# A new order of the opening work, later output projections, and one numerator moved out of the gate/up chunks

## The chip, the cores and the metric

The kernel runs on one core of a Trainium2 chip. The metric is the time of one execution on the device, in microseconds (us). The program is one instruction stream per engine: TensorE (PE) for matmuls, VectorE (DVE), ScalarE (ACT), GpSimd (POOL) and SyncE (SP), which issues most DMAs. Each engine takes its instructions in order, and the engines meet at semaphores.

## The reference

One token mixer and one feed-forward network read the same `x` (2048 tokens, 640 features), and a gate per token mixes them. Cut to what matters:

```
g = sigmoid((x * gate_w).sum(-1))
q, k, v = split(x @ wqkv)                    # 32 heads of 20
pq, pk = q @ w_phi[h], k @ w_phi[h]          # 20 x 20 for each head
phi = [softmax(p), softmax(-p)]              # for q and for k
kv, z = sum over tokens of phi_k * v, and of phi_k
o = (phi_q @ kv) / (phi_q @ z + 1e-6)
a = o @ wo
b = (gelu(x @ w_gate) * (x @ w_up)) @ w_down # 1728 hidden features
out = g * a + (1 - g) * b
```

The attention is linear: `kv` and `z` are sums over all tokens, so every key has to be done before the first output of attention.

## The kernel before, in words

Tokens are cut into 16 tiles of 128 and four slabs of 4 tiles. There are four stages, in an order written out by hand; a small helper (`_Sched`) adds to each instruction the semaphore waits that its buffers need. Everything below is issued from one Python loop, so the order of the calls is the order on each engine.

*Loads and start* (`loads`, then `attention_state` to its first `gram`). SyncE issues x for the first slab, the five row blocks of the v weights (L239), and then, one after the other, DMA transposes: x for tiles 4 and 5 (L224), the k weights `wkT` (L220), x for tiles 6 and 7, the q weights `wqT`, and x for the rest. ScalarE's queue loads `w_phi` (L235) and `gate_w` (L240). GpSimd makes the masks. VectorE multiplies `w_phi` with the masks into a block-diagonal `BD` (L307). TensorE does v of the first slab in steps by weight rows (L366), turns `gate_w` into a column (L316, copied by VectorE at L318), and does v of tiles 4 to 7 (`v_early`) and the keys of tiles 0 to 3 (`k_early`). `fold(kt, "k" or "q", banks, engine)` multiplies `w_phi` into the weights (L334): 6 matmuls into a pair of PSUM banks, then a copy by VectorE or ScalarE (L347, L349). A `k_early` needs all five k folds, a `pq` all five q folds. `proj` is the matmul loop behind them (its matmuls are recorded at L354).

*State* (the rest of `attention_state`). For each tile: keys and v, exponentials on ScalarE (L416), and on VectorE `k_norm`: sums over the 20 features of a head (L427), a reciprocal (L431), and two products (L436). `gram(t)` adds the tile to `kv` and `z` in PSUM banks 3 and 4 (L452), and `pq` makes the exponentials of the queries (`Eq`, L521). In this stage, once `columns` is set, a matmul is split into two halves of 64 columns.

*Gate/up* (`gateups`). For each slab 14 chunks of hidden features: 5 matmuls for gate and 5 for up (L354), gelu on ScalarE (L629), a product on VectorE (L631). During slab 0 the state is finished (`state`). During slab 1, after chunks 4 and 8, the *numerators* of tiles 0 and 1 are computed. A numerator `num(t)` is 20 matmuls into banks 2 to 5 (L657), a chain of eleven VectorE instructions (L673 to L686) that divides by the denominators and ends in `Og`, and a DMA transpose on SyncE's queue to `goT` (L689).

*Down* (`downs`). Tiles are done in pairs (`down_pair`). The contraction of 64 + 64 rows is split in two row halves that run side by side, one tile in each: a *step* is two matmuls (L713), one for each tile of the pair, in two different banks. The output columns are done in two parts of 320 (three parts of 256, 256 and 128 for the last pair), and each part has a first and a second half of the rows, so a pair has four *legs* (last pair: six). A leg is 14 steps (second half: 13) over `w_down`, followed by 5 steps over `wo`, which read `goT`. The second half's legs write the same banks as the first half's with rows exchanged, so they first wait for TensorE's own semaphore (`after=[("turn", bank)]`) of the first. Then the part is scaled by the gate and copied out (L726, L724), and the pair is stored (L737). A pair is 74 steps. `downs` counts the steps of a slab and places numerators after given ones: steps 1, 31, 61 and 91 of slab b carry tiles 4b+2 to 4b+5.

Of the kernel before, what the change touches and what calls it, by code (L numbers as in the profile page):

```python
# [3 lines left out]
P = 128  # L4
# [103 lines left out]
class _Kernel:  # L108
    S, D, H, DH, F = 2048, 640, 32, 20, 1728
# [98 lines left out]
    def loads(self):  # L208
# [13 lines left out]
        def xturn(t, n):  # L222
# [43 lines left out]
        for i in range(KD):  # L266
            n = self.HHI[i] - self.HLO[i] + 1
            base = P * i - DH * self.HLO[i]
            m = self.mask[:, i, 0:n]
            pool(lambda e, m=m: e.memset(m, 1.0), [("mask", i)])  # L270
            pool(lambda e, m=m, n=n, base=base: e.affine_select(
                m, m, pattern=[[-DH, n]], compare_op=ALU.is_ge, fill=0.0, base=base, channel_multiplier=1),
                [("mask", i)])
            pool(lambda e, m=m, n=n, base=base: e.affine_select(
                m, m, pattern=[[DH, n]], compare_op=ALU.is_ge, fill=0.0, base=DH - 1 - base, channel_multiplier=-1),
                [("mask", i)])
        for r in (0, 1):
# [143 lines left out]
            reads=[("ps", b0 + 1)], writes=[("gcol", t)])  # L421

    def k_norm(self, t):
        sc = self.sc
        se = t % self.NSE
        H, DH = self.H, self.DH
        sc.op("dve", lambda e: e.tensor_reduce(  # L427
            self.Dk[:, se, 0, :].rearrange("p (s h) -> p s h", h=H),
            self.Ek[:, se, :, :].rearrange("p s (h d) -> p s h d", d=DH), AX.X, ALU.add),
            reads=[("Ek", se, 0), ("Ek", se, 1)], writes=[("Dk", se)])  # L430
        sc.op("dve", lambda e: e.reciprocal(self.Dk[:, se, 1, :], self.Dk[:, se, 0, :]),  # L431
              reads=[("Dk", se)], writes=[("Rk", se)])
        for s in (0, 1):
            v = self.Ek[:, se, s, :].rearrange("p (h d) -> p h d", d=DH)
            r = self.Dk[:, se, 1, s * H:(s + 1) * H].unsqueeze(2).to_broadcast([P, H, DH])
            sc.op("dve", lambda e, v=v, r=r: e.tensor_tensor(v, v, r, ALU.mult),  # L436
                  reads=[("Rk", se)], writes=[("Ek", se, s)])
# [97 lines left out]
    def attention_state(self):  # L535
        NT = self.NT
        order = [(b, i) for b in range(self.NB) for i in range(self.KD)]
        sc = self.sc
        ones = self.nc.const_aps.tensor(1.0, [P, 512], BF16)
        for n in (512, 512, 512, 512, 512, 512, 128):  # L540
            sc.op("pe", lambda e: e.matmul(self.bank(0, n), ones[:, 0:P], ones[:, 0:n], start=True, stop=True),
                  writes=[("ps", 0)])
        vs, ve, xt = self.v_step, self.v_first_evac, self.x_transpose
        xt(0, 6, "d")
        xt(1, 7, "a")
        xt(2, 2, "d")
# [48 lines left out]
        for t in range(4, NT):  # L595
            if t < 8:
                self.k_early(t, 1)
            else:
                self.vk(t)
            self.k_norm(t)  # L600
            m = 2 * t - 2 if t < 8 else t + 5
            while n < m:
                if n == m - 1:
                    for g in range(g, t - 2):
                        self.gram(g)
                    g = t - 2
                self.pq(order[n][0], order[n][1], n)
                n += 1
# [80 lines left out]
        sc.dma("sp", lambda e: e.dma_start_transpose(self.goT[:, gs, :, :], self.Og[:, sl, :]),  # L689
               reads=[("Og", sl)], writes=[("goT", gs)], guard=old)  # L690

    def down_pair(self, t0, banks, widths):

        sc = self.sc
        ts = (t0, t0 + 1)
# [3 lines left out]
        last = t0 + 2 == self.NT  # L699
        os_ = t0 % 4  # L700

        def mm(r, j, h, c, opens, x, n):
            t = ts[j]
            tt, gs, bk, w0, a = t % 4, t % 8, banks[h][j], sum(widths[:h]), 64 * r
            w, end = widths[h], x == n - 1
# [7 lines left out]
            sc.op("pe", lambda e: e.matmul(self.bank(bk, w), lhs, rhs, start=opens and x == 0, stop=end and not opens,  # L713
                                           skip_group_check=True),
                  reads=rd, writes=[("ps", bk)] + ([("turn", bk)] if end else []), signal=end,
                  after=[("turn", bk)] if x == 0 and not opens else ())

        def evac(h):
            w0, w = sum(widths[:h]), widths[h]
# [17 lines left out]
            sc.dma("sp", lambda e: e.dma_start(rows[:, :, c0:c1], self.outsb[:, os_:os_ + 2, c0:c1]),  # L737
                   reads=[("outsb", os_ + j, k) for j in (0, 1) for k in hs], writes=[("out", t0, h)])

        for q in range(2 * nw):  # L740
            h, opens = q % nw, q < nw
            cs = list(range(NFC + 1 if opens else NFC)) + [NFC + 1 + k for k in range(KD)]
            for x, c in enumerate(cs):
                for r in (0, 1):
                    mm(r, r if opens else 1 - r, h, c, opens, x, len(cs))
                if x == len(cs) - 1 and not opens:
# [8 lines left out]
    def ffn(self):  # L755
# [10 lines left out]
        def downs(b, side):  # L766
            p = [pairs[(self.pn + k) % 2] for k in (0, 1)]
            n = 0
            for t in (4 * b, 4 * b + 2):
                final = t + 2 == self.NT  # L770
                for _ in self.down_pair(t, p + [(2, 3)] if final else p, (256, 256, 128) if final else (320, 320)):
                    n += 1
                    if n in side:
                        self.num(side[n])
# [69 lines left out]
```

The softmax here doesn't subtract the row's maximum and nothing guards it: scores larger than these inputs give would overflow.

## Time and profile before

| what | value |
|---|---|
| median of 8 runs | 287.98 us (287.43 to 288.28) |
| the profiled execution's own time | 288.28 us |
| its span, first to last instruction | 287.0 us |
| TensorE busy, loads and start, 0 to 29.60 us | 27.33 us of 29.60 |
| TensorE busy, state, 29.60 to 85.41 us | 55.81 us of 55.81 |
| TensorE busy, gate/up, 85.41 to 198.04 us | 111.73 us of 112.63 |
| TensorE busy, down, 198.04 to 284.20 us | 86.09 us of 86.16 |
| after the last matmul | 2.80 us |
| VectorE busy in the down stage | 55.73 us of 86.16 |
| granted TensorE clock | 1.00 throughout |

How to read it: all lines come from one profiled execution on the chip. A line of the timeline has the start, the busy time, engine, source line, operation, out<-in, and in brackets how long the engine was idle before and what ended that. The chain that ended last is the path from the last instruction back to whatever released it; "issue" in it is time in which the engine waited for nothing that the profile shows. SPq is SyncE's queue of DMA issues. A busy TensorE is not one at its peak, since matmuls overlap and their ends are modelled (a matmul of 512 columns is shown with 379 ns, but 50 of them take 10.74 us in the chain, 215 ns each); a few matmuls are missing from the records.

### The profile page before, as it was taken

The numbers are of one execution on the slowest core, as the hardware profiler recorded it, in microseconds if no ns is written. First come the engines' busy times: TensorE is split into PE (matmuls) and PEld (weight loads), VectorE is DVE, ScalarE is ACT, GpSimd is POOL, SyncE is SP. The second block draws the span as 40 slices with busy tenths as digits, with TensorE's granted clock in tenths as the row PEclk, the third lists the DMA queues.
The fourth block names the chain that finished last, engine by engine and source line by source line (L and its number), as shares of the span: only waits on it lengthen the run. The fifth ranks groups of instructions, "written<-read, shape, count | busy, mean of one in ns | idle before, by whom it ended". The sixth has DMA issues, their size and how long they took to land.

```text
span 287.0 us, 7005 instructions
## 1 busy us (share of the span) xinstructions
PE 281.0 (98%) x3017; PEld 185.8 (65%) x3032; DVE 174.8 (61%) x353; ACT 104.5 (36%) x199; POOL 5.3 (2%) x36
## 2 busy tenths in 40 slices
PE   8989999999999999999999999999999999999995
PEld 4666689999994444444444444445777777777785
DVE  1338999999977553567242334225883883883801
ACT  3357887677663322322323223321112112112111
POOL 7000000000000000000000000000000000000000
PEclk9999999999999999999999999999999999999999
DMA  8999994000002000011000000000232333332221
GB/s 220 211 199 273 362 365 143 0 2 2 2 0 48 0 0 0 3 24 23 2 0 0 0 2 0 0 2 0 26 93 62 34 48 94 48 55 83 53 72 48
DMA packets 36938, 18.67 MB, mean 65 GB/s; under 512 B 28971, under 2 KB 36395, under 8 KB 36907
## 3 DMA queue, kind: packets, MB, share of 16 engines
q1 hardware_dynamic: 36240, 18.19, 25.7%
q8 instruction: 24, 0.39, 0.6%
q10 hardware_dynamic: 666, 0.03, 0.2%
q14 instruction: 8, 0.06, 0.1%
HBM read 9.04 MB, written 2.62 MB: 41 GB/s over the span
## 4 chain that ended last, share of the span: by engine, by line
PE 93%; SPq 3%; DMA 2%; issue 1%; ACT 0%
PE ps L354 60%; PE ps L713 28%; PE ps L657 2%; DMA xT<-in_A_x_dram 2%; PE ps L452 2%; SPq L220 1%; PE ps L334 1%; SPq L239 1%; SPq L224 1%; SPq L216 0%; ACT outsb L726 0%
## 5 line engine op out<-in xcount | busy, mean ns | idle before, releaser
L354 PE MATMUL ps<-xT,wg_sb 128*128 128x512 bf16 (+1 forms) x265 | 63.8, 379 | 0.4 <-issue 0.2
L354 PE MATMUL ps<-xT,wu_sb 128*128 128x512 bf16 (+1 forms) x263 | 63.3, 379 | 0.5 <-DVE hT L631 0.2
L629 ACT ACTIVATE gl<-ps 128x512 bf16<-128x512 f32 x52 | 30.9, 596 | 73.1 <-PE ps L354 68.7
L631 DVE TENSOR_TENSOR hT<-ps,gl 128x512 bf16<-128x512 f32 x39 | 26.7, 690 | 38.3 <-PE ps L354 38.3
L713 PE MATMUL ps<-wd_sb,hT 64*128 64x320 bf16 x648 | 49.4, 296 | 0.0
L354 PEld LDWEIGHTS ps<-xT,wu_sb 128*128 128x128 bf16 (+1 forms) x270 | 26.5, 99 | 29.8 <-DVE hT L631 0.5
L354 PEld LDWEIGHTS ps<-xT,wg_sb 128*128 128x128 bf16 (+1 forms) x270 | 26.2, 99 | 29.0 <-ACT gl L629 0.2
L354 PE MATMUL ps<-w,xT 128*64 128x512 bf16 (+6 forms) x398 | 41.6, 325 | 1.1 <-DMA xT<-in_A_x_dram 0.9
L726 ACT ACTIVATE outsb<-ps,Gm 128x320 bf16<-128x320 f32 (+2 forms) x31 | 14.5, 515 | 72.4 <-PE ps L713 72.4
L354 PEld LDWEIGHTS ps<-w,xT 128*64 128x64 bf16 (+1 forms) x400 | 35.6, 107 | 6.0 <-DMA xT<-in_A_x_dram 1.1
L713 PEld LDWEIGHTS ps<-wd_sb,hT 64*128 64x128 bf16 x648 | 31.0, 94 | 12.2 <-issue 0.4
L713 PE MATMUL ps<-wo_sb,goT 64*128 64x320 bf16 (+2 forms) x340 | 27.8, 288 | 0.0
L354 PE MATMUL ps<-xT,wq 128*64 128x512 bf16 (+1 forms) x184 | 25.9, 380 | 0.1
L436 DVE TENSOR_TENSOR Ek<-Ek,Dk 128x640 bf16<-128x640 bf16 x32 | 25.0, 821 | 0.6
L684 DVE TENSOR_TENSOR O<-ps,RH 128x640 bf16<-128x640 f32 x32 | 24.8, 815 | 0.0
L427 DVE TENSOR_REDUCE Dk<-Ek 128x64 f32<-128x1280 bf16 x16 | 23.7, 1478 | 0.0
L416 ACT ACTIVATE Ek<-ps 128x640 bf16<-128x640 f32 x32 | 20.7, 703 | 3.5 <-PE ps L354 3.5
L521 ACT ACTIVATE Eq<-ps 128x512 bf16<-128x512 f32 x40 | 21.6, 607 | 0.7 <-PE ps L354 0.4
L631 DVE TENSOR_TENSOR xT<-ps,gl 128x512 bf16<-128x512 f32 x13 | 9.0, 691 | 18.2 <-PE ps L354 18.2
L713 PEld LDWEIGHTS ps<-wo_sb,goT 64*128 64x128 bf16 x340 | 16.1, 94 | 5.4
L354 PEld LDWEIGHTS ps<-xT,wq 128*64 128x64 bf16 (+1 forms) x185 | 15.3, 108 | 2.9
L713 PE MATMUL ps<-wd_sb,xT 64*128 64x320 bf16 (+2 forms) x270 | 16.7, 269 | 0.0
(69 smaller groups left out, 173.0 us busy)
## 6 DMA issues: line engine op xcount, KB each, us to landing
out_dram<-outsb SPq DMA_DIRECT2D x7, 320.0 KB, 2.3
wd_sb<-in_B_w_down_dram SPq DMA_DIRECT2D x1, 2080.0 KB, 14.3
wg_sb<-in_B_w_gate_dram SPq DMA_DIRECT2D x1, 1120.0 KB, 5.7
wu_sb<-in_B_w_up_dram SPq DMA_DIRECT2D x1, 1120.0 KB, 8.2
wg_sb<-in_B_w_gate_dram SPq DMA_DIRECT2D x1, 960.0 KB, 10.0
wu_sb<-in_B_w_up_dram SPq DMA_DIRECT2D x1, 960.0 KB, 10.5
w<-in_A_wqkv_dram SPq DMA_DIRECT2D x5, 160.0 KB, 4.3
wo_sb<-in_A_wo_dram SPq DMA_DIRECT2D x1, 800.0 KB, 9.5
```

The lines of the kernel that those rows point to most:

```text
L354: self.sc.op("pe", lambda e: e.matmul(self.ps[a:z, bank * 512 + c0:bank * 512 + c0 + n], lhs[:, a:z], rhs, start=first, stop=fin), reads=r ...
L416: self.sc.op("act", lambda e, s=s, scale=scale: e.activation(self.Ek[:, se, s, :], self.ps[:, o:o + self.D], AF.Exp, scale=scale), reads=[ ...
L427: sc.op("dve", lambda e: e.tensor_reduce(self.Dk[:, se, 0, :].rearrange("p (s h) -> p s h", h=H), self.Ek[:, se, :, :].rearrange("p s (h d ...
L436: sc.op("dve", lambda e, v=v, r=r: e.tensor_tensor(v, v, r, ALU.mult), reads=[("Rk", se)], writes=[("Ek", se, s)])
L452: sc.op("pe", lambda e: e.matmul(self.ps[a:a + 64, b * 512 + c:b * 512 + c + 2 * nf], va[:, lo:lo + 64], self.Ek[:, se, :, f0:f0 + nf], st ...
L521: sc.op("act", lambda e, s=s, scale=scale: e.activation(self.Eq[:, s, i, b * self.BT:(b + 1) * self.BT], self.bank(bank), AF.Exp, scale=sc ...
L629: sc.op("act", lambda e: e.activation(self.gl[:, slot, :], self.bank(banks[0]), AF.Gelu_apprx_tanh), reads=[("ps", banks[0])], writes=[("g ...
L631: sc.op("dve", lambda e: e.tensor_tensor(hT, self.bank(banks[1]), self.gl[:, slot, :], ALU.mult), reads=[("ps", banks[1]), ("gl", slot)], ...
L657: sc.op("pe", lambda e: e.matmul(self.bank(bk)[:, o0:o0 + w], self.Eq[a:a + 64, s, i, t * P:(t + 1) * P], self.KV[a:a + 64, i, s, :], star ...
L684: dve(lambda e, o=o, f=f, s=s: e.tensor_tensor(o, V[s][:, :, :, 0:DH], f, ALU.mult), rb + [key(6 + s)], [("O", s, sl)], guard=old)
L713: sc.op("pe", lambda e: e.matmul(self.bank(bk, w), lhs, rhs, start=opens and x == 0, stop=end and not opens, skip_group_check=True), reads ...
L726: sc.op("act", lambda e: e.activation(dst, self.bank(bk, w), AF.Copy, scale=g), reads=rd, writes=wr)
```

## The change

It changes three places. In `loads`, the two DMAs on ScalarE's queue are moved behind GpSimd's masks in the program, and the first of them now waits for mask 1 instead of the identity matrix. In `attention_state`, the order of folds, v and keys is new, with other banks; `k_norm` is cut into `k_sums` and `k_scale`, and the sums of tile 0 are taken early. In the down stage, `down_pair` gets a parameter `late`, true for tiles 0 and 1 alone: there all four `w_down` legs come first, then the `wo` legs, both halves of a part in a row. In all other pairs the first half's `w_down` legs of all parts come first, then the first half's `wo` legs, then the second half as before. Numerator 1 leaves the gate/up chunks; numerators 1 to 5 are placed in slab 0 after steps 1, 31, 61, 91 and 121, and the later slabs keep theirs.

```diff
@@ loads
-        sc.dma("act", lambda e: e.dma_start(
-            self.wphi_sb[:, :, :], self.wphi.rearrange("h d f -> (h d) f").rearrange("(i p) f -> p i f", p=P)),
-            reads=["ident"], writes=["wphi"])
...
-        sc.dma("act", lambda e: e.dma_start(self.gz[0:KD, :], self.gw.rearrange("(k p) -> k p", p=P)), writes=["gz"])
...
+        sc.dma("act", lambda e: e.dma_start(
+            self.wphi_sb[:, :, :], self.wphi.rearrange("h d f -> (h d) f").rearrange("(i p) f -> p i f", p=P)),
+            reads=[("mask", 1)], writes=["wphi"])
+        sc.dma("act", lambda e: e.dma_start(self.gz[0:KD, :], self.gw.rearrange("(k p) -> k p", p=P)), writes=["gz"])
@@ attention_state
         f = self.fold
-        self.v_early(4, 6)
-        self.v_early(5, 0)
+        ve, ke = self.v_early, self.k_early
+        ve(4, 6)
+        ve(5, 0)
         f(0, "k", (2, 3), "d")
         f(1, "k", (4, 5), "a")
-        self.v_early(6, 6)
-        f(2, "k", (2, 3), "d")
-        f(3, "k", (4, 5), "a")
-        f(4, "k", (0, 1), "d")
-        self.v_early(7, 6)
-        self.k_early(0, 2)
+        f(2, "k", (6, 7), "d")
+        f(3, "k", (0, 1), "a")
+        f(4, "k", (2, 3), "d")
+        ve(6, 4)
+        ke(0, 6)
+        self.k_sums(0)
+        ve(7, 0)
+        ke(1, 2)
         f(0, "q", (4, 5), "d")
         f(1, "q", (6, 7), "d")
-        self.k_early(1, 0)
+        ke(2, 0)
         f(2, "q", (4, 5), "d")
-        f(3, "q", (6, 7), "d")
-        self.k_early(2, 2)
+        f(3, "q", (2, 3), "d")
+        self.proj(3, 640, 384, 6, 128, ["wk2"])
         f(4, "q", (4, 5), "d")
-        self.k_norm(0)
-        self.k_early(3, 0)
+        self.proj(3, 1024, 257, 7, 0, ["wk2", "wgate"])
+        self.k_evac(3, 6)
+        self.k_scale(0)
         self.k_norm(1)
-        self.pq(0, 1, 1)
-        self.pq(0, 0, 0)
-        self.pq(0, 3, 3, 0)
+        self.pq(0, 1, 1, 0)
+        self.pq(0, 0, 0, 1)
+        self.pq(0, 3, 3, 2)
@@ down_pair
-        for q in range(2 * nw):
-            h, opens = q % nw, q < nw
-            cs = list(range(NFC + 1 if opens else NFC)) + [NFC + 1 + k for k in range(KD)]
...
+        wos = [NFC + 1 + k for k in range(KD)]
+        down = (list(range(NFC + 1)), list(range(NFC)))
+
+        def leg(h, half, cs, first, fin, enter, leave):
...
+        if late:
+            for half in (0, 1):
+                for h in range(nw):
+                    yield from leg(h, half, down[half], half == 0, False, half == 1, True)
+            for h in range(nw):
+                yield from leg(h, 0, wos, False, False, True, True)
+                yield from leg(h, 1, wos, False, True, True, True)
+        else:
+            for h in range(nw):
+                yield from leg(h, 0, down[0], True, False, False, False)
+            for h in range(nw):
+                yield from leg(h, 0, wos, False, False, False, True)
+            for h in range(nw):
+                yield from leg(h, 1, down[1] + wos, False, True, True, True)
@@ ffn
         def first_nums(idx):
-            if idx in (4, 8):
-                self.num(idx // 4 - 1)
+            if idx == 4:
+                self.num(0)
...
-        at = (1, 31, 61, 91)
+        at = (1, 31, 61, 91, 121)
+        nums = ((1, 2, 3, 4, 5), (6, 7, 8, 9), (10, 11, 12, 13), (14, 15))
...
-            downs(b, {at[k]: 4 * b + 2 + k for k in range(4 if b < 3 else 2)})
+            downs(b, dict(zip(at, nums[b])))
```

In `leg`, `enter` puts a wait for the banks' last leg ahead of its first matmul, `leave` lets its last matmul signal, and `fin` ends with the copy out.

More of the change, by code (lines that the diff above doesn't have):

```diff
@@ L423, in k_norm, with k_sums @@
     def k_norm(self, t):
+        self.k_sums(t)
+        self.k_scale(t)
+    def k_sums(self, t):
         sc = self.sc
@@ L430, in k_norm, with k_scale @@
             reads=[("Ek", se, 0), ("Ek", se, 1)], writes=[("Dk", se)])
+    def k_scale(self, t):
+        sc = self.sc
+        se = t % self.NSE
+        H, DH = self.H, self.DH
         sc.op("dve", lambda e: e.reciprocal(self.Dk[:, se, 1, :], self.Dk[:, se, 0, :]),
@@ L690, in num, with down_pair @@
                reads=[("Og", sl)], writes=[("goT", gs)], guard=old)
-    def down_pair(self, t0, banks, widths):
+    def down_pair(self, t0, banks, widths, late):
         sc = self.sc
@@ L700, in down_pair, with mm @@
         os_ = t0 % 4
-        def mm(r, j, h, c, opens, x, n):
+        def mm(r, j, h, c, start, stop, enter, leave):
             t = ts[j]
             tt, gs, bk, w0, a = t % 4, t % 8, banks[h][j], sum(widths[:h]), 64 * r
-            w, end = widths[h], x == n - 1
+            w = widths[h]
             if c <= NFC:
@@ L712, in mm @@
                 rd = [("goT", gs), "wo"]
-            sc.op("pe", lambda e: e.matmul(self.bank(bk, w), lhs, rhs, start=opens and x == 0, stop=end and not opens,
+            sc.op("pe", lambda e: e.matmul(self.bank(bk, w), lhs, rhs, start=start, stop=stop,
                                            skip_group_check=True),
-                  reads=rd, writes=[("ps", bk)] + ([("turn", bk)] if end else []), signal=end,
-                  after=[("turn", bk)] if x == 0 and not opens else ())
+                  reads=rd, writes=[("ps", bk)] + ([("turn", bk)] if leave else []), signal=leave,
+                  after=[("turn", bk)] if enter else ())
         def evac(h):
@@ L738, in evac @@
                    reads=[("outsb", os_ + j, k) for j in (0, 1) for k in hs], writes=[("out", t0, h)])
-        for q in range(2 * nw):
-            h, opens = q % nw, q < nw
-            cs = list(range(NFC + 1 if opens else NFC)) + [NFC + 1 + k for k in range(KD)]
+        wos = [NFC + 1 + k for k in range(KD)]
+        down = (list(range(NFC + 1)), list(range(NFC)))
+        def leg(h, half, cs, first, fin, enter, leave):
             for x, c in enumerate(cs):
                 for r in (0, 1):
-                    mm(r, r if opens else 1 - r, h, c, opens, x, len(cs))
-                if x == len(cs) - 1 and not opens:
+                    mm(r, (r, 1 - r)[half], h, c, first and x == 0, fin and x == len(cs) - 1, enter and x == 0,
+                       leave and x == len(cs) - 1)
+                if fin and x == len(cs) - 1:
                     evac(h)
                 yield None
+        if late:
[12 more added lines that the diff above has]
+                yield from leg(h, 1, down[1] + wos, False, True, True, True)
     NUMB = 2
@@ L770, in downs @@
                 final = t + 2 == self.NT
-                for _ in self.down_pair(t, p + [(2, 3)] if final else p, (256, 256, 128) if final else (320, 320)):
+                for _ in self.down_pair(t, p + [(2, 3)] if final else p, (256, 256, 128) if final else (320, 320),
+                                        t == 0):
                     n += 1
```

## The prediction

> **What bounds the kernel now.** First the page: who is busy, and the chain that ended last.
>
> ```profile
> PE 281.0 (98%) x3017; PEld 185.8 (65%) x3032; DVE 174.8 (61%) x353; ACT 104.5 (36%) x199; POOL 5.3 (2%) x36
> ...
> PE 93%; SPq 3%; DMA 2%; issue 1%; ACT 0%
> ```
>
> TensorE sets the time, and it runs almost without a pause. The change removes no matmul (the order of its instructions holds the same ones), so it can only close pauses, open new ones, or move work between places of different price. The pauses come from the chain in order of time, around 9 to 18 us:
>
> ```profile
> 10.03 5.34 DMA xT<-in_A_x_dram
> 15.37 0.05 issue
> 15.41 1.53 PE ps L354 x10
> 16.95 0.94 PE ps L334 x18
> 17.89 0.13 issue
> ```
>
> v of tile 6 (L354) waits for its transposed x, which lands at 15.37; folds 2 to 4 of k (18 matmuls of L334, 0.94 us) come after it. The list of waits puts this pause at 0.9 us, the longest on TensorE. The next one, in the timeline at 26 to 30 us:
>
> ```profile
> 27.93 1.56 DVE L436 TENSOR_TENSOR Ek<-Ek,Dk 128x640 bf16<-128x640 bf16 x2
> ...
> 29.57 0.35 PEld L452 LDWEIGHTS ps<-Ek,vaug 128*64 128x64 bf16 x11 [0.47 <-DVE Ek L436]
> ```
>
> The first gram waits for VectorE's normalised keys; on the matmuls themselves this is about 0.2 us (the pq matmuls would have ended at 29.4, gram starts at 29.60). Then the chain among gate/up chunks and in the down stage:
>
> ```profile
> 124.97 0.21 issue
> 125.18 3.19 PE ps L354 x14
> 128.37 0.50 PE ps L657 x20
> ...
> 198.28 0.39 PE ps L657 x20
> 198.67 4.07 PE ps L713 x60
> 202.75 0.39 PE ps L657 x20
> ```
>
> A numerator (L657, 20 matmuls) costs 0.39 us between down matmuls. Among gate/up it costs more: in the timeline, groups of five matmuls start 1.08 us apart (126.04, 127.12), but 1.68 apart with numerator 1 between them (127.12, 128.80), so 0.60. A down step is two matmuls: 4.07 / 30 = 0.136 us. Last, a numerator's way to goT, in VectorE's timeline and in the transposes to goT:
>
> ```profile
> 207.80 0.36 DVE L673 RECIPROCAL RH<-ps 128x32 f32<-128x32 f32 x1
> ...
> 211.51 0.49 DVE L686 TENSOR_TENSOR Og<-O,O 128x640 bf16<-128x640 bf16 x1
> ```
>
> ```profile
> L689 SPq DMA_TRANSPOSE goT<-Og x1: 1203/1203/1203, 212.1 to 212.1; - x1
> ...
> DMA to landing us min/median/max: 2.6/2.6/2.6
> ```
>
> Numerator 4 ends on TensorE at 207.60 (207.21 + 0.39 in the chain); its transpose is issued at 212.07 and lands 2.56 later. So goT is 7.03 us behind its numerator at best. The same view gives 3.2 to 4.2 us for other landings: 3.2 at 203.1, 3.7 at 224.8, 3.5 at 233.7, 3.6 at 246.5.
>
> **What the Trainium skill says.** *TensorE: Matmul & The Clock Gate*, "Single matmul latency": (398 + N) / 2.4 ns, 299 ns for N = 320; the page's row for L713 has 296. The same page, "The cost: per-tile semaphore tail": 25 + 4.7 per tile + 26.3 per increment, 87 ns for two; nothing in this trace shows it. *Runtime: NRT & Kernel Launch*, "Instruction fetch mechanics": instructions come in blocks of 16 KiB by DMA, 256 at a time, mostly hidden. The page of before has such a queue (q8 instruction: 24 packets, 0.39 MB, 16 KiB each); that these are what lengthens some goT landings is my guess. *DMA: Bandwidth & Descriptors*, "Issuing engines are not separate DMA queues": ScalarE's DMAs share the 16 engines with SyncE's. The page agrees in that w_phi (25 KB) takes 6.0 us to land beside the v rows.
>
> **The change part by part**, against the profiled execution: 288.28 us, span 287.0, so 1.28 outside it. The median of the runs is 287.98, 0.30 lower; I add my sum to the median.
>
> 1. *w_phi and gate_w later.* Their two ScalarE DMAs now wait for the second mask on GpSimd (about 2.8 us) instead of being issued at 1.69 and 2.19. ScalarE's next work is at 4.87, so its queue loses nothing. w_phi lands about 1.2 later, at 8.9; five BD products (1.2 us) end at 10.1 instead of 8.9. Folds need BD at 13.7, and the copy L318 behind BD frees a bank for v 4 at 11.25: hidden, with 0.9 us to spare. If w_phi came 2 us later still, v 4 would wait about 1 us. Gain: the first v row lands at 5.4 and v begins at 5.52; w_phi's packets leave its way, 0 to 0.3 us. But v 6 waits for x at 15.37 in any case, so what is gained before it is lost there. I take 0.
>
> 2. *k folds in a row, new order up to gram 0.* Folds 2 to 4 fill the pause: +0.94. Fold 4 uses fold 0's banks, which VectorE frees at 14.33 + 0.82 = 15.15, so it ends near 15.5 and v 6 starts up to 0.1 later: -0.05. The 0.13 at 17.89 goes too (v 7 waited there for v 6's copy in its bank; now 2.7 us lie between): +0.08. From v 6 on the same matmuls follow, 8.4 us for v 7, keys 0 to 3 and five q folds, so pq starts near 25.2 instead of 26.2. I followed each bank by hand: the tightest is q fold 4, whose banks VectorE frees at 24.25 for a start at 24.3. The sum over keys 0 (L427, 1.48 us) moves into VectorE's pause at 19.7; the last q copy ends at 25.8, then reciprocal 0.55 and two products 1.56: keys 0 are ready at 27.95, gram 0 starts at 28.4. With the sum left in place it would be 29.4, and this gain would be gone. So gram 0 no longer waits: +0.13. Together **-1.1 us** (bounds -0.8 and -1.4). Behind it TensorE has no pause until 124 in which it could be given back.
>
> 3. *Numerator 1 from gate/up to down step 1.* 0.60 - 0.39 = **-0.2 us**. The 0.21 at 124.97 belongs to numerator 0, which stays.
>
> 4. *Late output projection for tiles 0 and 1.* The wo legs now stand two and two on one bank pair, and the second leg waits for the end of the first with nothing between: 0.296 + 0.087 - 0.068 (the pace it replaces) = 0.31. Twice: **+0.6 us** (bounds 0.45; 0.9 if a weight load of 0.094 is exposed too). TensorE's queue is in order, so all else on it waits.
>
> 5. *goT 1.* Numerator 1 after step 1, needed at step 55: 53 steps x 0.136 + 0.39 (numerator 2) = 7.60 us. The numerator at that place before took 198.67 to 203.09 + 3.2, 7.62. **+0.1 us** (0 to 1.0, if it lands after 4.2).
>
> 6. *goT 3.* Numerator 3 moves from step 31 to 61. Tiles 2 and 3 start at step 75; two down legs of 14 steps first, so goT 3 is needed at step 103: 41 steps, 5.58, + numerator 4, 0.39, + one wait of part 4, 0.31 = 6.28 us. It takes 4.47 + 2.56 + 0.05 = 7.08 at best: 0.8 us. With a slow landing of 3.5, 8.02: 1.7 us. All four first transposes of a slab of four tiles were slow before, of the three in numerator 3's place (212.1, 233.7, 255.4) two. I take **+1.7 us** (0.7 to 2.0). Nothing hides it.
>
> 7. *Other tiles.* Their wo legs come later, and both halves keep at least ten matmuls (0.68 us) between, more than part 4's 0.38: 0. goT 5 (step 121) has 55 steps + 0.39 = 7.87 against 7.03 to 8.0: 0. SyncE's queue keeps goT 3 ahead of the first output. The last legs, which set the tail of 2.8 us, are unchanged.
>
> Sum: -1.1 - 0.2 + 0.6 + 0.1 + 1.7 = +1.1, so 287.98 + 1.1 = **289.1 us**.
>
> **Rivals.** (a) *Quick landings*: goT 3 lands after 2.56 and goT 1 in time: -1.3 + 0.6 + 0.8 = +0.1, 288.1, no change. For it: nine of sixteen landings took under 3 us. (b) *The waits of the down stage are small* and the start decides: two waits at 0.23 (no tail), goT 3 0.5, start and numerator -1.6 with the x chain pulled forward by w_phi's absence (its queue had 0.2% of sixteen engines, 0.57 us each): -0.65, 287.3, faster. It decides once the start gains more than down loses. Against it: x is issued by SyncE at 10.03, long after w_phi, and 6.28 against 7.08 leaves little doubt. (c) *Both goT late* (goT 1 by 1.0): +2.0 to +2.4, 290.2.
>
> **The numbers.** Forecast 55% (own range 288.6 to 289.9), (a) 25%, (b) 10%, (c) 10%. A measurement of this kernel tells about 0.2% (0.6 us) from no change. Slower by more: the forecast and (c), less a tip of the first: 0.64; same: (a) and that tip: 0.26; faster: (b), 0.10. Range 287.5 to 290.2: it leaves out half of (b) and of (c).
>
> **What would show it.** v 6 at 15.4 with no k fold after it, gram 0 at 28.4 with no wait; one L657 group among gate/up; two pauses of 0.3 us between wo legs near 206; a pause of 0.8 or 1.7 at the first wo matmul of tiles 2 and 3, ended by a DMA to goT. Wrong if that last pause is missing, or gram 0 stays at 29.6.

## The result and the profile after

The changed kernel takes 290.93 us (median of 11 runs, 290.49 to 291.57), the kernel before 288.00 us in the 32 runs made beside it: ratio 1.0102, 95% interval 1.0089 to 1.0114, so 2.9 us slower. The forecast was 289.1, its range ended at 290.2. The profiled execution after has 291.33 us of its own and a span of 290.1 (before 288.28 and 287.0, so +3.1 in the spans). Beside three of the experiments below, 8 of the 59 runs of the kernel before took 290.6 to 291.3 us at a granted clock of 0.994, and none of those experiments' own runs did; without the eight, these three ratios (0.9959, 1.0028 and 1.0034) would be 0.001 higher. Line numbers have moved: down matmuls are L726 (before L713), numerators L670 (L657), `Og` L699 (L686), the transposes to `goT` L702 (L689), `gram` L461 (L452).

The page after, busy time and then the chain that ended last, by engine and by line:

```profile
PE 282.8 (97%) x3018; PEld 186.7 (64%) x3032; DVE 175.2 (60%) x353; ACT 104.5 (36%) x199; POOL 5.3 (2%) x36
...
PE 25%; DMA 1%; issue 0%; DVE 0%; ACT 0%; SPq 0%
PE ps L726 23%; PE ps L670 2%; DMA goT<-Og 1%; DVE Og L699 0%; ACT outsb L739 0%; SPq L42 0%
```

TensorE still sets the time, but its share fell from 98 to 97%. The second line is the finding: the chain no longer runs back on TensorE to the start. It leaves TensorE at a transpose to `goT` and goes on to VectorE. The list of waits of TensorE (line, releaser, sum, times, longest) agrees:

```profile
PE ps L726 <- DMA goT<-Og: 2.3, 2, 1.3
...
PEld ps L670 <- DVE O L697: 0.4, 1, 0.4
```

The second line, a numerator's weight load that waits for VectorE, comes back below. Before, no wait for `goT` stood there. The wait for `xT` (0.9) is gone.

*Where the 3.1 us are.* I compare four points on TensorE, after against before. The first gram starts at 29.22 (29.60): -0.38. Gate/up starts at 85.22 (85.57), down at 197.00 (197.97), so gate/up takes 111.78 instead of 112.40: -0.62, of which numerator 1's 0.39 comes back in the down stage. The last matmul ends at 287.24 (284.20), so down takes 90.24 instead of 86.23: +4.01. After it 2.86 instead of 2.80.

*The start*, TensorE and VectorE in the timeline:

```profile
3.71 2.31 PE L293 MATMUL ps<-ident,xtok 128*128 128x128 bf16 x20
...
14.32 1.95 PE L334 MATMUL ps<-BD,wkT 128*128 128x140 bf16 x30
16.32 5.39 PE L354 MATMUL ps<-w,xT 128*128 128x512 bf16 x39
...
26.93 1.56 DVE L445 TENSOR_TENSOR Ek<-Ek,Dk 128x640 bf16<-128x640 bf16 x2
...
29.22 0.35 PEld L461 LDWEIGHTS ps<-Ek,vaug 128*64 128x64 bf16 x11 [0.42 <-issue]
```

The five k folds run in one group (x30) and v of tile 6 follows without a pause. Keys 0 are ready at 28.49 (26.93 + 1.56), before gram 0 could start: what stands ahead of it in its bracket is "issue" and no longer "DVE Ek". But the first line, 20 transposes by matmul in 2.31 us, is slower than before (1.55, see the last section), and TensorE reached the v rows 0.30 later and left them 0.57 later than before.

*The down stage*, TensorE's wo legs of tiles 0 to 3, and VectorE's `Og` of numerator 3:

```profile
205.13 0.30 PE L726 MATMUL ps<-wo_sb,goT 64*128 64x320 bf16 x1
206.41 1.36 PE L726 MATMUL ps<-wo_sb,goT 64*128 64x320 bf16 x13 [0.98 <-DMA goT<-Og]
...
212.40 0.49 DVE L699 TENSOR_TENSOR Og<-O,O 128x640 bf16<-128x640 bf16 x1 [0.44 <-DVE O L697]
...
214.22 0.30 PE L726 MATMUL ps<-wo_sb,goT 64*128 64x320 bf16 x1
...
215.86 1.53 PE L726 MATMUL ps<-wo_sb,goT 64*128 64x320 bf16 x19 [1.35 <-DMA goT<-Og]
```

Each step is two matmuls, one for each tile. The even tile's starts (205.13, 214.22), the odd tile's comes late (206.41, 215.86): `goT` 1 and `goT` 3 are awaited. At the usual pace of 0.068 per matmul (half a step), the first wait is worth 206.41 - 205.13 - 0.068 = 1.21, the second 215.86 - 214.22 - 0.068 = 1.57. The chain in order of time shows the second and one that I had not on my list, numerator 6:

```profile
212.40 0.50 DVE Og L699
...
212.97 2.84 DMA goT<-Og
215.81 0.05 issue
215.86 2.66 PE ps L726 x37
...
222.81 0.03 issue
222.84 0.56 PE ps L670 x20
```

Numerator 6 (222.84) waits 0.26 for VectorE to leave numerator 5's PSUM banks. The two turn waits (a second wo leg waits for the end of the first on the same banks) are read from TensorE's single records. The second legs start at 207.32 and 209.33, 0.356 and 0.387 after the last start before them. At the first, one matmul stands before the wait, since `goT` 1's wait left the two tiles half a step apart, so 0.356 - 0.068 = 0.29 is wait; at the second a whole step does, so 0.387 - 0.136 = 0.25. With these the down stage adds up: numerator 1 0.39 + turns 0.54 + `goT` 1 1.21 + `goT` 3 1.57 + numerator 6 0.26 = 3.97, measured 4.01.

### The profile page after: what moved, and what is told of

It reads as the page before. It is cut to its first block, busy times and chain, and to the rows that moved or that the text cites. A ratio compares the mean times of both kernels' runs of the same rounds, so it can differ in the third digit from the quotient of the medians.

```text
span 290.1 us, 7008 instructions
## 1 busy us (share of the span) xinstructions
PE 282.8 (97%) x3018; PEld 186.7 (64%) x3032; DVE 175.2 (60%) x353; ACT 104.5 (36%) x199; POOL 5.3 (2%) x36
## 3 DMA queue, kind: packets, MB, share of 16 engines
HBM read 9.04 MB, written 2.62 MB: 40 GB/s over the span
## 5 line engine op out<-in xcount | busy, mean ns | idle before, releaser
L726 PE MATMUL ps<-wd_sb,hT 64*128 64x320 bf16 x648 | 48.8, 296 | 0.0
L726 PEld LDWEIGHTS ps<-wd_sb,hT 64*128 64x128 bf16 x648 | 31.4, 94 | 12.1 <-issue 0.4
L726 PE MATMUL ps<-wo_sb,goT 64*128 64x320 bf16 (+2 forms) x340 | 27.4, 288 | 2.5 <-DMA goT<-Og 2.3
L726 PEld LDWEIGHTS ps<-wo_sb,goT 64*128 64x128 bf16 x340 | 16.0, 94 | 8.9 <-DMA goT<-Og 3.0
L726 PE MATMUL ps<-wd_sb,xT 64*128 64x320 bf16 (+2 forms) x270 | 16.0, 269 | 0.0
## 6 DMA issues: line engine op xcount, KB each, us to landing
wd_sb<-in_B_w_down_dram SPq DMA_DIRECT2D x1, 2080.0 KB, 14.4
```

## The experiments

My theory after this: the start gains what it can; the down stage loses by `goT` 1 and 3, by the turn waits and by numerator 6; and `goT` 1 lands late because a block of TensorE's instructions (page: q8 instruction, 24 packets of 16 KiB) is fetched while its transpose is under way. Rivals: the turn waits are the costly part; or the first transpose of a slab is late as such. The runs were made on several chips; each ratio is taken with the kernel before on its own chip (its median is 288.08 to 288.73 there), so ratios are compared and not medians. None of them leaves out any of the reference's work. The "clock" of some expectations is TensorE's: in the traces, the first matmuls run at about half their later pace, and when they speed up differs from execution to execution (last section).

### The two halves of the change

Start alone (the change's loads, `k_sums`/`k_scale` and order, with the old `down_pair` and numerators), and down alone (the old start with the new `down_pair` and numerators):

```diff
# start alone, against the change
-    def down_pair(self, t0, banks, widths, late):
+    def down_pair(self, t0, banks, widths):
...
-            if idx == 4:
-                self.num(0)
+            if idx in (4, 8):
+                self.num(idx // 4 - 1)
```

> The kernel before with the change's loads, folds and early sums alone; down stage and numerators as before. Theory (all of the loss is made in the down stage, the start gains): 0.9 us faster than before, 287.1, the first gram at 28.4 to 28.7 when TensorE's clock is up before the v steps as in the profile of before, near 29.2 when it comes up as late as in the profile after. Rival (the new start itself is what brings the clock up late, and so gains little): 0.4 us faster or none, 287.6 to 288.0, first gram again at 29.2.

Measured: 287.60 us, ratio 0.9974 (0.9960 to 0.9987), so -0.75 us (-1.15 to -0.37), between the theory's 0.9 and the rival's 0.4: the runs do not tell the two apart. Gram 0 at 29.22; no wait for `goT`.

> The kernel before with the change's down stage and the moved numerator 1 alone. Theory: slower by what the profile after shows there, 4.0 us in the down stage less 0.6 in gate/up: +3.4, and up to 0.5 more or less by where the landings of goT fall; 291.4. Rival (part of the loss in the change comes from the two halves together): less than +2.5.

Measured: 291.63 us, ratio 1.0107 (1.0075 to 1.0139), so +3.1 us. `goT` 1 lands 4.23 after its issue and costs 1.27, `goT` 3 costs 1.77, the turns 0.29 and 0.25, numerator 6 0.26. The halves add up to +2.35, with the change's +2.93 within their intervals. The whole loss is in the down stage.

### The turn waits taken away

The late wo legs in the order part, part, part, part, so that another part's leg stands between two on the same banks:

```diff
-            for h in range(nw):
-                yield from leg(h, 0, wos, False, False, True, True)
-                yield from leg(h, 1, wos, False, True, True, True)
+            for half in (0, 1):
+                for h in range(nw):
+                    yield from leg(h, half, wos, False, half == 1, True, True)
```

> The changed kernel, but in the late pair the wo legs go first half of both parts, then second half of both, so that ten matmuls lie between a leg and the one that waits for it. Theory (each of the two waits for TensorE's own end costs 0.3): 0.6 us faster than the changed kernel, so +2.3 against before, the two pauses of 0.3 us gone, the two waits for goT still there (1.2 and up to 0.3 more of the second, since less lies ahead of it). Rival (the time is only shifted into the wait for goT 3): as the changed kernel, +2.9.

Measured: ratio 1.0094 (1.0059 to 1.0129). The interval holds the change's 1.0102 (the rival) and also 1.0080 (the theory), so the trace has to decide. The turn waits are gone, but the waits for `goT` grew (1.34 and 1.98), and a new one came, in the timeline of this kernel:

```profile
209.21 1.78 ACT L739 ACTIVATE outsb<-ps,Gm 128x320 bf16<-128x320 f32 x4 [12.55 <-PE ps L726]
209.79 0.09 PEld L726 LDWEIGHTS ps<-wd_sb,hT 64*128 64x128 bf16 x1 [0.27 <-ACT outsb L739]
...
210.21 1.88 PEld L726 LDWEIGHTS ps<-wd_sb,hT 64*128 64x128 bf16 x30 [0.33 <-ACT outsb L739]
```

The next pair's first leg follows ten matmuls after the first part's last, and ScalarE has not copied its two banks out. By the pace of 0.068 this costs 0.52. So in this profile the 0.54 of the turns is lost again, and more: 0.52 at ScalarE's copy, 0.13 at `goT` 1, 0.41 at `goT` 3. The last is not the turns' time come back, as the rival had it: the new wait lies between numerator 3 and its deadline as the second turn did, so the deadline came no earlier after the numerator (it came 0.26 later). It is the landing that took 3.42 instead of 2.84.

### Where the instruction blocks fall

In the trace's DMA packets of queue q8 I read when each 16 KiB packet starts; on average some 255 TensorE instructions lie between two. For all transposes to `goT` in the down stage of the change:

```
goT                   1    2    3    4    5    6    7    8    9   10   11   12   13   14   15
next packet after  2.11  6.7 0.31  4.1  6.5 2.03  4.9 0.43  2.8 1.88  5.1 0.64  3.4 2.18  5.5
issue to landing   4.17 2.60 2.84 2.57 2.57 4.31 2.62 2.97 2.58 4.23 2.57 4.30 2.62 4.23 2.57
```

Every transpose here with a packet within 2.2 us behind its issue is late, every other takes 2.57 to 2.62. But a coincidence in time is not a cause. So I moved the packets and left the work as it is: TensorE gets three more waits (on GpSimd, ScalarE and VectorE) in each gate/up chunk of slabs 1 to 3, which are always satisfied when it gets there (none of them is in this kernel's list of waits).

```diff
+        if b and c < 13:
+            for k in ("pool", "act", "dve"):
+                self.nc.tensor.wait_ge(sc.engs[k]["sem"], 1 + self.gn % 7)
```

> The changed kernel with some hundred extra waits on TensorE's queue among the gate/up chunks of slabs 1 to 3, all on semaphore values reached long before, so that nothing waits but TensorE has more instructions and fetches its blocks of 256 at other places. Theory (goT lands late, 2.8 to 4.3 us after its issue, where an instruction fetch falls between 0.3 and 2.2 us behind the issue, and after 2.6 otherwise): the late landings are no longer those of numerators 1, 3, 6, 8, 10, 12 and 14 but others, and each fits that window again; if numerator 1 is out of it, its wait falls from 1.2 to under 0.1 us, if numerator 3 is, its wait is 0.7 to 1.3. Rival (the place in the slab makes the landing late, for instance the first transpose after a pause): numerators 1, 6, 10 and 14 land after 4.2 us as before, and the waits stay.

Measured: 288.97 us, ratio 1.0026 (1.0013 to 1.0040): 2.2 us less than the change, by adding instructions. First `goT` 1 in the change, then in this kernel (its transposes are L705), from the views of one transpose:

```profile
L702 SPq DMA_TRANSPOSE goT<-Og x1: 1201/1201/1201, 202.2 to 202.2; - x1
...
DMA to landing us min/median/max: 4.2/4.2/4.2
```

```profile
L705 SPq DMA_TRANSPOSE goT<-Og x1: 1692/1692/1692, 201.9 to 201.9; - x1
...
DMA to landing us min/median/max: 2.9/2.9/2.9
```

The packet now starts 0.34 behind the issue instead of 2.11, and the landing is 2.89 instead of 4.17. TensorE (L729 here) runs through the wo legs of tile 1 and still waits at tile 3:

```profile
204.84 1.38 PE L729 MATMUL ps<-wo_sb,goT 64*128 64x320 bf16 x14
...
212.68 0.30 PE L729 MATMUL ps<-wo_sb,goT 64*128 64x320 bf16 x1
...
214.05 1.53 PE L729 MATMUL ps<-wo_sb,goT 64*128 64x320 bf16 x19 [1.08 <-DMA goT<-Og]
```

Others became late instead: `goT` 4 took 4.38 (packet at +2.11), 7 took 4.25, where the change had 2.57 and 2.62; nothing waits for those. The rival "the first in a slab is late as such" fell: `goT` 6, 10 and 14 landed after 2.81, 3.18 and 3.02, where the change had 4.31, 4.23 and 4.23. And since adding waits to TensorE's queue moved the packets, they are TensorE's blocks. Of the 2.2 us, the waits for `goT` 1 and 3 give 1.21 + 0.27; the rest turned up later, at the very end (last experiment).

A smaller shift, with one extra wait per chunk instead of three, the one on GpSimd:

> The changed kernel with one extra wait per gate/up chunk of slabs 1 to 3 on TensorE's queue, on values reached long before: 39 instructions, half of the shift in the run with three. Theory of the instruction fetch: 39 more entries put the fetch near goT 1 about 1.3 us earlier, at 202.9 to 203.2, still inside the window of goT 1 (issued at 202.0), so its landing stays late (3 to 4.3) and its wait 0.3 to 1.2; the next, 7.5 us on, comes at 211 to 212, ahead of or just at goT 3's issue near 212.5, so goT 3 lands after 2.6 and its wait is 1.3: 0.3 to 0.8 faster than the changed kernel. Rival (landings depend on the place in the slab, not on the count of instructions): as the changed kernel, goT 1 after 4.2, goT 3 after 2.8.

Measured: ratio 1.0028 (1.0009 to 1.0047). `goT` 1 lands after 3.58 (packet at +0.65) and costs 0.61, half of the change's. `goT` 3 lands after 2.88 with a packet at +0.12, where I had expected none: a miss, the block of that place did not move out of its way. This wait's 0.60 and 0.7 at the end (last experiment) make up the 1.3 between the spans (288.8 against 290.1). The ratio says 2.1. Part of the other 0.8 is the eight runs of the kernel before that are named with the result; what the rest is stays open.

### Numerator 1 put back, the late legs kept

```diff
-            if idx == 4:
-                self.num(0)
+            if idx in (4, 8):
+                self.num(idx // 4 - 1)
...
-        at = (1, 31, 61, 91, 121)
-        nums = ((1, 2, 3, 4, 5), (6, 7, 8, 9), (10, 11, 12, 13), (14, 15))
+        at = (1, 31, 61, 91)
+        nums = ((2, 3, 4, 5), (6, 7, 8, 9), (10, 11, 12, 13), (14, 15))
```

> The changed kernel with numerator 1 back after chunk 8 of gate/up slab 1 and numerators 2 to 5 at steps 1, 31, 61 and 91 of slab 0; new start and late wo legs kept. Theory (the loss is made of goT waits that the moved numerators cause; the late legs cost only two waits for TensorE itself): no pause that a DMA to goT ends, two pauses of 0.3 left, so 0.7 faster by the start and 0.6 slower by the legs: within 0.3 of before, 287.8 to 288.4. Rival (the legs themselves, not the numerators' places, make the waits): 2 us slower or more.

Measured: 288.20 us, ratio 0.9989 (0.9976 to 1.0002). No wait for `goT` is left and numerator 6 does not wait either; the two turn waits stay with 0.25 each. So all of the change's loss but the turn waits comes from moving numerator 1 into the down stage, which pushes numerators 2 to 5 one place back.

### The other way round: late legs for all of slab 0

The late order for tiles 2 and 3 too, with the leg order of the run without turn waits:

```diff
-                                        t == 0):
+                                        b == 0):
```

> The changed kernel with the wo legs interleaved as in the run without the two waits for TensorE itself, and with tiles 2 and 3 late as well: all four w_down legs before their wo legs, so goT 3 is needed at step 129 instead of 103. Theory: the wait for goT 3 (1.6) is gone, the wait for goT 1 (1.2) stays, a wait for ScalarE's copy of 0.4 stands behind each of the two pairs: against before -0.75 (start) - 0.2 + 1.2 + 0.8 + 0.3 = +1.3, so 1.6 faster than the changed kernel. Rival (the wait moves on to goT 5 of the next slab): less than 0.8 faster than the changed kernel.

Measured: ratio 1.0034 (1.0016 to 1.0052). The wait for `goT` 3 is gone (its deadline is 26 steps later), that for `goT` 1 stays at 1.20 (landing 4.16), and ScalarE's copy costs 0.52 at 210.1 and again at 221.5, where I had expected 0.4. Better than the change, still slower than before.

### The start taken apart

The new order with the loads as before, and the new loads with the order as before:

```diff
# new order alone, against start alone: the two DMAs go back behind xload("sp", 2)
+        sc.dma("act", lambda e: e.dma_start(
+            self.wphi_sb[:, :, :], self.wphi.rearrange("h d f -> (h d) f").rearrange("(i p) f -> p i f", p=P)),
+            reads=["ident"], writes=["wphi"])
```

> The kernel before with the new order of folds, v and keys and the early sums, but w_phi and gate_w loaded where they were. Theory (the order alone makes the start's gain; w_phi's place does nothing): as the start alone, 0.7 faster than before. Rival 1 (w_phi behind the v rows brings the clock up late): the clock is up before the v steps, and 1.2 faster. Rival 2 (w_phi's packets ahead of the v rows delay them): v steps start later, 0.4 faster.

Measured: 287.84 us, ratio 0.9978 (0.9967 to 0.9988), -0.64 us. In its profiled execution x for tiles 6 and 7 lands only at 16.46, and v of tile 6 waits in spite of the folds:

```profile
13.81 1.95 PE L334 MATMUL ps<-BD,wkT 128*128 128x140 bf16 x30
16.74 2.45 PE L354 MATMUL ps<-w,xT 128*128 128x512 bf16 x17 [0.97 <-DMA xT<-in_A_x_dram]
```

> The kernel before with w_phi and gate_w loaded behind the masks, nothing else. Theory: nothing, within 0.2 of before, since v of tile 6 waits for its own transposed x. Rival 1 (it brings the clock up late in the transposes): 0.3 to 0.6 slower, v steps from 5.8. Rival 2 (it brings the x transposes forward): 0.3 to 0.7 faster, x of tiles 6 and 7 landing at 14.5 instead of 15.4.

Measured: ratio 1.0005 (0.9990 to 1.0020), gram 0 at 29.69. The later load of `w_phi` is worth nothing alone, and its absence takes nothing away that can be measured.

The start alone, with the sums of keys 0 left in `k_norm(0)`:

```diff
-        self.k_sums(0)
...
-        self.k_scale(0)
+        self.k_norm(0)
```

> The new start alone, but with the sums over keys 0 back in front of their reciprocal instead of in VectorE's pause. Theory (VectorE would then be late for the first gram by up to 1 us): gram 0 waits for VectorE 0.4 to 1.0 us, and the run is 0.4 to 1.0 slower than the start alone, 288.0 to 288.6. Rival (there is slack enough): as the start alone, 287.6.

Measured: ratio 1.0006 (0.9990 to 1.0021), 0.9 us worse than start alone: the whole gain is gone.

```profile
26.13 1.47 DVE L431 TENSOR_REDUCE Dk<-Ek 128x64 f32<-128x1280 bf16 x1
...
28.23 1.56 DVE L445 TENSOR_TENSOR Ek<-Ek,Dk 128x640 bf16<-128x640 bf16 x2
...
29.86 0.35 PEld L461 LDWEIGHTS ps<-Ek,vaug 128*64 128x64 bf16 x11 [1.28 <-DVE Ek L445]
29.89 0.46 PE L461 MATMUL ps<-Ek,vaug 128*64 128x120 bf16 x11 [0.82 <-DVE Ek L445]
```

The sum (1.47) stands on VectorE's way to gram 0, and TensorE's matmuls wait 0.82 for it.

### A version that beats both kernels, and the end

Numerator 1 three chunks before the down stage instead of in it, all pairs in the change's other leg order:

```diff
+        def last_num(idx):
+            if idx == 9:
+                self.num(1)
...
-        gateups(3, none)
+        gateups(3, last_num)
```

with `late` False everywhere and numerators 2 to 5 after steps 1, 31, 61 and 91.

> The changed kernel with numerator 1 behind chunk 9 of gate/up slab 3 (by count, not by number), three chunks or 6.5 us ahead of the down stage, numerators 2 to 5 at steps 1, 31, 61 and 91, and no late pair (all pairs have both first-half w_down legs, then the wo legs). Theory (what counts is the distance from a numerator to the wo leg that needs it, not the stage it sits in): no wait for goT at all, as the start alone, 0.7 faster than before, 287.3 to 287.9. Rival (the new leg order of the pairs that are not late costs something itself): 0.3 or more slower than the start alone.

Measured: 287.67 us beside 288.73, ratio 0.9959 (0.9943 to 0.9976), against 0.9974 for start alone: within their intervals the same. No wait for `goT`; the chain is TensorE's again, by engine and by line:

```profile
PE 97%; DMA 1%; issue 0%; ACT 0%
PE ps L354 61%; PE ps L726 28%; PE ps L670 2%; PE ps L366 2%; PE ps L461 2%; PE ps L334 1%; DMA xtok<-in_A_x_dram 1%; PE ps L293 1%; ACT outsb L739 0%; PE ps L316 0%
```

The rest of the 2.2 us of the three extra waits lies behind the last matmul: 2.86 us to the end of the span in the change, 2.1 in the kernel with the three extra waits. There the last instruction block starts 2.9 us before the last output's DMA; in the change it starts at 286.94, 0.7 before the issue. The last run joins both: this version with the three extra waits.

> This kernel has numerator 1 three chunks before the down stage and no late legs, plus the three extra waits of TensorE per gate/up chunk of slabs 1 to 3, already satisfied when they are reached; none changes the work. Theory (an instruction block on its way delays the last output too): in the change the last block sets out at 286.94 us, just before the last output is issued at 287.66, and that output lands 2.38 us later; with the extra waits alone the last block set out 2.9 us before the output's issue, which landed after 1.65. Here the last block should set out over 1.5 us before the last output, the output land within 1.65 to 1.7 instead of the 2.12 us of the same kernel without the extra waits, and the time after TensorE's last matmul end shrink from 2.5 to about 2.07 us; no goT wait of TensorE. The ratio to before is then lower than 0.9959 by some 0.0015, about 0.994, if the extra waits themselves cost nothing. Rival (the short tail belonged to the late legs of that kernel, or the extra waits cost as much): the last output takes 2.1 us or more, and the ratio is 0.996 or above.

Measured: 287.00 us beside 288.08, ratio 0.9960 (0.9945 to 0.9975). The last output in the version without the extra waits, and then with them:

```profile
L750 SPq DMA_DIRECT2D out_dram<-outsb x1: 851/851/851, 284.5 to 284.5; - x1
...
DMA to landing us min/median/max: 2.1/2.1/2.1
```

```profile
L753 SPq DMA_DIRECT2D out_dram<-outsb x1: 372/372/372, 283.8 to 283.8; - x1
...
DMA to landing us min/median/max: 1.6/1.6/1.6
```

The landing is as the theory had it (the last block 2.7 us ahead of the issue), and what follows the last matmul is 2.1 instead of 2.6 us. The other traces agree: where the last q8 packet starts 0.3 to 0.8 us before the last output's issue, that output takes 2.09 to 2.54 (eleven traces), and where it starts 1.7 us or more before, 1.65 (three, all with extra waits). In the eleven, the packet starts 0.15 to 0.54 behind the issue of the output before, so the last one may be late only because that one is; this is not shown. The ratio is not lower than without the waits, as the rival had it; 0.0015 is no more than the interval's half width, so the gain at the end is shown in the trace and not in the runs' times.

## Why the prediction was wrong, step by step

1. *w_phi later: 0.* Right (1.0005 alone). `w_phi` itself landed at 7.4 and not at 8.9, since it took 4.5 from its later issue instead of 6.0.
2. *The new order: -1.1, bounds -0.8 and -1.4.* Too large: -0.75 (-1.15 to -0.37). The mechanism stands: the folds fill the pause, and without the early sums the gain is gone by 0.9, where my text had 1.0. But gram 0 is at 28.4 in no trace with the whole new order: at 28.76 to 29.25 in seven, at 29.49 to 29.70 in three (two of them with x late). Three terms were missing. The folds wait twice for their banks (0.07 and 0.13, where I had 0.05 for one). v of tile 6 still waits for x in two of these ten traces, by 0.8 and 1.0: x landed between 14.4 and 16.5 in different executions, while I treated the 15.37 of one execution as the kernel's. And the first matmuls ran slow for longer in several of these executions (last section).
3. *Numerator 1: -0.2.* Right: -0.62 in gate/up, +0.39 in down.
4. *Turn waits: +0.6.* Near: 0.29 + 0.25. The price of the Trainium skill (*TensorE: Matmul & The Clock Gate*, "The cost: per-tile semaphore tail") that went into it, 0.087, is of the right size here: from the modelled end of the leg before, TensorE stood idle 0.06 and 0.09. But what the wait replaces is the pace of a whole step, 0.136, and not 0.068: 0.296 + 0.091 - 0.136 = 0.25. That one of the two also lies ahead of `goT` 3's deadline, I had in step 6 (as 0.31).
5. *goT 1: +0.1 (0 to 1.0).* **This is the step that failed**: 1.21. My sum took a landing of 3.2, which is what the numerator at that place had before. That number was no property of the place: in the trace of before the packet started 0.67 behind that issue, in the change 2.11, and the landing was 4.17. I had named these packets as a guess, and had landings up to 4.2 in my list, and still took a single one as the value. The bound above was worked out from 4.2 and was short by 0.2, for a second reason: I began the numerator's way where the chain ends it, with the end of its last matmul (198.67), but counted the steps to the deadline from start to start. Counted so throughout, the numerator ended at 198.50 before, and its way to the issue was 4.59 and not 4.42 (4.65 in the change, 197.54 to 202.19). 4.65 + 4.17 + 0.05 - (205.13 - 197.54) - 0.068 = 1.21.
6. *goT 3: +1.7.* The size is right (1.57), but by luck: two errors cancel. I took numerator 4's row for the way from the numerator to the issue, 4.47; numerator 3's own is 4.98 here (207.99 to 212.97) and was 4.99 before (202.97 to 207.96). Of these 0.5, 0.17 is the mixed counting of step 5, and 0.35 is VectorE's pause ahead of this numerator's `Og`, 0.44 where the others have 0.09. And I took a slow landing of 3.5 where it was 2.84. 4.98 + 2.84 + 0.05 - (214.22 - 207.99) - 0.068 = 1.57. With a quick landing of 2.57 the kernel with three extra waits still has 1.30, not the 0.8 of rival (a).
7. *Other tiles: 0.* Right for `goT` 5. But I looked only at who waits for `goT`, not at who waits for the banks of a numerator: between step 121 of slab 0 and step 1 of slab 1 lie 28 steps and not 30, and numerator 6 comes 0.26 early for VectorE.

In sum the terms measure -0.75 - 0.2 + 0.54 + 1.21 + 1.57 + 0.26 = +2.6, against 2.93. Of the 1.8 us by which the forecast's +1.1 fell short, `goT` 1 makes 1.1, the start 0.35 and numerator 6 0.26. Rival (c), both `goT` late, was the case that came true, and it was priced at 290.2 with one chance in ten. What I had wrong about it was also the weight: which transposes are late hangs on where the instruction stream's blocks fall, which every edit shifts. In the trace of before one of sixteen landings takes over 4 us, in the change five of sixteen, so one trace did not tell the share either. The Trainium skill (*Runtime: NRT & Kernel Launch*, "Instruction fetch mechanics") calls the fetch mostly hidden. For TensorE, no trace here speaks against that; for other queues' DMAs it is not hidden: 0.2 to 1.9 us on a transpose (last section).

## What to carry to other kernels

A DMA's time to landing in one trace is a sample, so price a deadline with the longest landing that the trace shows for such a DMA, and ask what else starts beside it, an instruction block included; the next edit will move that block. Moving a piece of work one place back in a row of equal slots moves all behind it: check each one's deadline, and each one's buffers too. A wait taken away can bring out another behind it: here 0.54 of turn waits went and 0.52 at ScalarE's copy came.

## What the runs showed of the hardware

- A transpose to `goT` that is under way when an instruction block is fetched is late, the more so the later the block comes. In the fourteen traces (before, after and twelve runs) there are 224 transposes from `Og` to `goT`. From issue to landing, by when a 16 KiB packet of q8 starts behind the issue (28 with a packet of the other instruction queue, q14, 1.9 to 2.8 behind the issue are left out):

```
packet of q8 starts   transposes   landing after
not from -1.4 to +2.6     99       2.55 to 2.63
-1.36 to +0.01            10       2.55 to 2.60
+0.10 to +0.36             9       2.79 to 3.11
+0.36 to +0.70            22       2.94 to 3.60
+0.70 to +1.00            11       3.28 to 3.91
+1.00 to +1.50             6       3.60 to 4.26
+1.50 to +2.12            22       4.03 to 4.43
+2.12 to +2.40            17       2.55 to 2.62 (8), 4.12 to 4.51 (9)
```

  A packet that starts ahead of the issue does nothing, and at the other edge, where the transpose has nearly landed, it is all or nothing. An 8 KiB packet of q14 alone does it too: numerator 0's transpose has one at +1.9 to +2.0 in every trace and takes 3.20 to 3.22 each time, numerator 12's has one at +2.07 in three traces and takes 3.58 or 3.59. Right behind the issue it does not: in eight traces numerator 3's has one at +0.1 and takes 2.57 or 2.58. Moving the packets moves the lateness (shown by the runs with extra waits). Through which resource they meet was not tried.
- VectorE pauses 0.44 us ahead of numerator 3's `Og` (shown in the fence of the down stage above) in all fourteen traces, wherever that `Og` starts between 206.57 and 212.63, and not at its neighbours (0.09 to 0.11). An 8 KiB packet of q14 starts 0.66 to 0.96 us behind the start of that `Og` (at 208.06 before, 213.09 after); that a block of VectorE's own instructions ends there is only argued.
- The time at which the first matmuls come to full rate differs between executions, from 3.7 to 6.8 us (before 4.4, after 6.4). Before it the transposes of the first lines start 0.107 apart, after it 0.056. It is TensorE's clock: eleven of the fourteen traces hold a record of the granted clock at 1.00, and it begins where the pace changes, at 4.41 before, at 6.35 after, between 3.57 and 6.71 in all. Time without a record is shown as 1.00 on the page, which is why the page does not show it; that the clock stands at half until then is inferred from the pace. In the three traces with `w_phi`'s load in its old place the record begins at 3.57 to 4.41, in the eight others at 3.95 to 6.71, two of them at 3.95 and 4.03, so whether the move has a part in it is not settled. What sets the time was not tried. In the profile after, the 20 transposes took 2.31 us instead of 1.55, and v of the first slab ended 0.57 later: a start's gain read from a single pair of profiles is uncertain by about that for this alone.
